# A gated attention with a token mixer, one core: the small row group takes all its weight blocks from transposes

## The chip, the cores and the metric

The kernel runs on one core of a Trainium2 chip. Its engines each work through a list of instructions of their own, in order: TensorE (PE in the profile; its weight loads are listed as PEld), VectorE (DVE), ScalarE (ACT), GpSimd (POOL) and SyncE (SP), which here does nothing but issue DMAs. The metric is the device time of one execution in microseconds (us). Of the kernel before, three executions took 765.38, 765.40 and 765.44 us, with a median of 765.40 us.

## The reference

For each of 8 batches, with S = 3200 tokens and D = 256:

```
scores = (1 / S) * z @ z.T                 # z is 3200 x 64
x      = u * (relu(scores) ** 2 @ v)       # 3200 x 256
wq, wk = x @ w_q, x @ w_k                  # 3200 x 64
mixed  = (1 / 8) * wq @ (wk.T @ x)         # the einsums, in this order of products
out    = relu(mixed) @ w_out               # 3200 x 256
```

The matrix of scores is symmetric, since z is multiplied by its own transpose. The kernel uses this: a block of weights relu(s)^2 between token tiles i and j is the transpose of the block between j and i.

## The kernel before

**Tiles and groups.** The 3200 tokens of a batch are 25 tiles of 128. The rows of the output are taken in seven row groups: groups 0 to 5 have four tiles (512 rows), and the small group, number 6 (`LASTG`), has tile 24 alone (128 rows). For each row group the second product sums over all 25 token tiles: weights block (stationary) times v (moving, 256 columns), into two accumulators `acc` in PSUM, one for the first two row tiles of the group and one for the other two.

**Score tiles and pairs.** A score tile (an entry of the list `tiles`, lines 253 to 281) is 512 columns: for a big group, one token tile against the group's 512 rows; for the small group, four token tiles against its 128 rows, in four matmuls of 128 columns. Two score tiles make a pair. A pair's contraction is 64 long, so its two tiles run side by side, on the upper and the lower 64 rows of TensorE (`scores`, line 296; the matmul is line 307). A pair is then evicted with ReLU and a scale into `g` (`first_stage`: line 321 on DVE, line 319 on ACT), squared into `at` in float16 (`second_stage`: line 332 on POOL, line 330 on ACT), and read by the second product two steps later (`LAG = 2`). There are 11 buffers for `at`, three of two PSUM banks for scores and other short products, and seven for `g`.

**Turned blocks.** Blocks are not computed twice where `is_turned` says so (line 237): for groups gi < gj, with gj at most gi + 2, or the pair (0, 4). Such blocks are computed for group gi, and a DMA transpose from `at` to a shared buffer `tt` (line 351, issued from SP) makes the block that group gj needs. There are seven shared buffers; the plan in lines 285 to 293 gives each new block of groups the buffer whose last read is earliest. For the small group the list `FOR_SMALL` (line 242) names the big groups whose blocks come turned, into buffers of their own, `ts3` to `ts5`; these come from the score tile of token tile 24, which each of the big groups computes anyhow, as the last of its list. The other token tiles of the small group are computed as score tiles of its own: 13 token tiles, so four score tiles of which the last holds tile 24 alone. That makes 114 score tiles in a batch and 912 in all (`NTILE`).

**Steps.** Lines 1028 to 1231 are a loop over numbered steps `k`. A step issues the score matmuls of up to `n = 6` score tiles (three pairs), evicts them, squares the pairs of the step before, and runs a share of the second product of the current row group. The first `heading` pairs are issued at the step's start, the rest between the products. A group takes 25/8, so some three or four steps; the first of them *begins* the group, and the last *closes* it. When a group closes, `gate` (line 488) reads both accumulators: DVE multiplies the first with u (line 507), ACT copies the second to SBUF (line 506), and POOL multiplies that (line 509). The next group's first product into the same accumulators has to wait for that.

**Extra work in a step.** A step can carry one extra piece of the later stages: a *mix* (line 657, in the place of one score pair, so n = 4), a *key* step (`keys_and_heads`, which makes the projections of an x group and the head sums of an older one), or a *projection* (`project`, output products). Where a group begins, the extra piece is put before the group's own first products; elsewhere it goes between them. Which step carries what is decided by rules (`mix_due`, `key_due`, and the condition for `projecting`), and for the steps that stand in the table `chosen` (line 911) by its letters. The table `heading_more` changes the number of heading pairs of a step.

**SP's queue.** SP issues, in one order: loads of u, v and z (v and z come as `piece` in float32, line 147, three buffers, and are cast later by POOL or ACT, line 151, three to five steps after their load), the transposes of x (`xT_sb`, line 518), keys (`kx`, line 551), z (line 176), the turned blocks (line 351) and the stores of the output.

Of the kernel before, what the change touches and what calls it, by code (L numbers as in the profile page):

```python
# [16 lines left out]
def kernel(  # L17
# [219 lines left out]
    def is_turned(gi, gj):  # L237
        return gi < gj < LASTG and (gj <= gi + FAR or (gi, gj) == (0, 4))

    FOR_SMALL = (3, 4, 5)

    def group_of(ti):
        return max(gi for gi in range(NG) if starts[gi] <= ti * P)
# [8 lines left out]
    for b in range(B):  # L254
        for gi in range(NG):
# [4 lines left out]
            if gi == LASTG:  # L260
                own = [t for t in own if group_of(t) not in FOR_SMALL]
            if b == 0 and gi == 0:
# [18 lines left out]
    NTILE = len(tiles)  # L281

    tt_of, tt_free = {}, [(-1.0, n) for n in range(7)]
    for b, gi, tis in tiles:
        gj = group_of(tis[0])
        if is_turned(gi, gj) and (b, gi, gj) not in tt_of:
# [37 lines left out]
    def second_stage(p0, g, on_act):  # L326
# [7 lines left out]
        for h, (b, gi, tis) in enumerate(tiles[p0 : p0 + 2]):  # L334
            for i, ti in enumerate(tis):
                made[b, gi, ti] = (at, h * W + i * widths[gi])
            gj = group_of(tis[0])
            if is_turned(gi, gj) or (gj == LASTG and gi in FOR_SMALL):
                blocks.append((b, gi, gj, tis[0] - starts[gj] // P, 1, h * W, (h + 1) * W))
# [526 lines left out]
    def group_begun(k, b, gi):  # L866
# [40 lines left out]

    heading_more = {165: -1}  # L910
    chosen = {
        18: "k", 19: "p", 20: "p", 21: "m", 35: "k", 36: "p", 38: "p", 101: "p", 142: "mp",
        147: "k", 148: "m", 149: "m", 159: "mp", 161: "p", 163: "m"
    }

    def mix_due(k):
# [72 lines left out]
    def opening(order):  # L989
        sc, g = {}, {}  # L990
        for word in order.split():
            what, n, by = word[0], int(word[1:2]), word[2:]
            if what == "z":
                cast_first(n, int(by[0]), by[1])
            elif what == "t":
                turn_first(n)
            elif what == "c":
                place_first(n, by)
            elif what == "v":
                load_first_v(*[(0, 4), (12, 6), (18, 7), (4, 8)][n])  # L1000
            elif what == "s":
                sc[n] = scores(2 * n)
            elif what == "e":
                g[n] = first_stage(2 * n, sc.pop(n), by == "A")
            elif what == "q":
                each(second_stage(2 * n, g.pop(n), by == "A"))
            elif what == "w":
                warm(2 * int(word[1:]))
            elif what == "u":
                load_u(0, 0)  # L1010
            elif what == "m":
                ti = [t for x in tiles[2 * n : 2 * n + 2] for t in x[2]]
                for fn in whole(second_product(0, 0, ti, n == 0, False)):
                    fn()
        return [(2 * n, g[n]) for n in sorted(g)]
# [3 lines left out]
    waiting = opening(OPENING)  # L1019
    made_by = [4, 10, 16]  # L1020
    produced, consumed, k = 16, 6, 3
# [6 lines left out]
    while groups:  # L1028
# [3 lines left out]
        n = 6  # L1032
# [7 lines left out]
        if mix_due(k):  # L1040
# [1 line left out]
            mixed_at[0] = k  # L1042
            mixing += (mix(*mixing),)
            n = 4
        n = min(n, NTILE - produced)
        pairs = list(range(produced, produced + n, 2))
        on_lanes = k >= 3 and len(pairs) + bool(mixing) >= 2
        keying = not mixing and key_due(k)
# [26 lines left out]
            stage(p0, sc)  # L1075
        if len(waiting) == 3:
            second_on_act = [False, True, k % 2 == 0]
        else:
            second_on_act = [False, True]
        seconds = [(p0, g, a) for (p0, g), a in zip(waiting, second_on_act) if g is not None]  # L1080
# [149 lines left out]
        waiting = staged  # L1230
# [123 lines left out]
```

## Time and profile before

The profiled execution took 765.49 us, of which its span, from the first to the last instruction, is 763.7 us; so some 1.8 us lie around the span, and the execution is 0.09 us above the median.

| engine | busy us | share of the span | instructions |
|---|---|---|---|
| PE | 754.3 | 99% | 12888 |
| ACT | 551.1 | 72% | 651 |
| POOL | 537.1 | 70% | 351 |
| DVE | 461.9 | 60% | 458 |

In the rows that follow, a group of instructions is shown as line, engine, operation, tiles (out<-in), shapes and count; behind the first bar stands the time in which at least one of them ran and the mean of one in ns, behind the second the engine's idle time before them. "64*128" is the part of TensorE's array that a matmul takes, so two such matmuls can run at once. A timeline row gives the start, the length, the engine, the instruction and, in brackets, the idle time before it. In the rows of stretches the first column is the stretch, then its length, and for each engine busy time and instructions, then the granted clock of TensorE, the share of the DMA engines and GB/s.

### The profile page before, as it was taken

How to read it: one execution, taken by the hardware profiler on the slowest of the kernel's cores; microseconds unless marked ns; L12 is line 12 of the kernel's file. 1: busy time of each engine (PE TensorE's matmuls, PEld its weight loads, DVE VectorE, ACT ScalarE, POOL GpSimd, SP SyncE). 2: the span in 40 equal slices, each digit the busy share in tenths (PEclk: the TensorE clock that was granted, in tenths of full speed). 3: DMA queues.
4: the chain of work that ended last, by engine and by line, in shares of the span. 5: the costliest groups of instructions: out<-in, count | busy, mean ns of one | idle time of the engine just before them, and what ended most of it. 6: DMA issues, size and time to landing. Idle time of an engine off the chain costs nothing.

```text
span 763.7 us, 29059 instructions
## 1 busy us (share of the span) xinstructions
PE 754.3 (99%) x12888; PEld 618.0 (81%) x12888; DVE 461.9 (60%) x458; ACT 551.1 (72%) x651; POOL 537.1 (70%) x351
## 2 busy tenths in 40 slices
PE   9999999999999999999999999999999999999996
PEld 6777888888888887888888888888878888888884
DVE  7655676546755567555665557656566565755534
ACT  8666776677767777687776877759777697776555
POOL 7897797768766678676787668866688665854540
PEclk9999999999999999999999999999999999999999
DMA  8999789887999969997899998999899999798636
GB/s 178 189 197 219 187 187 192 174 181 160 206 196 233 219 166 185 221 235 195 214 177 219 243 195 181 158 228 265 135 223 189 228 250 156 161 222 193 176 74 262
DMA packets 289614, 150.23 MB, mean 197 GB/s; under 512 B 265168, under 2 KB 268752, under 8 KB 289488
## 3 DMA queue, kind: packets, MB, share of 16 engines
q1 hardware_dynamic: 288768, 146.48, 91.2%
q0 software_dynamic: 576, 1.64, 1.1%
q8 instruction: 100, 1.64, 0.9%
q14 instruction: 26, 0.21, 0.1%
q10 hardware_dynamic: 144, 0.26, 0.1%
HBM read 59.38 MB, written 26.21 MB: 112 GB/s over the span
## 4 chain that ended last, share of the span: by engine, by line
PE 97%; DVE 2%; issue 0%; DMA 0%; ACT 0%; DVEq 0%; ACTq 0%
PE acc L369 72%; PE sc L307 12%; PE fo L369 5%; PE qk L369 5%; PE mx L657 1%; DVE x_sb L507 1%; DVE fo L1312 0%; DVE g L321 0%; PE ztp L130 0%; DMA z<-in_z_dram 0%; PE qk L610 0%; DVE zT L136 0%; PE xtx L634 0%; PE hd L644 0%; ACT fo L1316 0%
## 5 line engine op out<-in xcount | busy, mean ns | idle before, releaser
L321 DVE TENSOR_SCALAR g<-sc 128x1024 f32<-128x1024 f32 x329 | 400.5, 1223 | 240.5 <-PE sc L307 225.9
L332 POOL TENSOR_TENSOR at<-g 128x1024 f16<-128x1024 f32 x229 | 431.4, 1893 | 131.1 <-DVE g L321 106.5
L369 PE MATMUL acc<-v_sb,at 64*128 64x256 f16 (+1 forms) x7187 | 461.8, 269 | 1.6 <-DVE x_sb L507 0.5
L369 PEld LDWEIGHTS <-at 64*128 64x128 f16 (+1 forms) x7187 | 353.9, 94 | 86.9 <-PE acc L369 25.4
L330 ACT ACTIVATE at<-g 128x1024 f16<-128x1024 f32 x227 | 236.1, 1056 | 14.3 <-DVE g L321 7.2
L369 PE MATMUL acc<-v_sb,tt 64*128 64x256 f16 x2552 | 178.7, 269 | 0.0
L307 PE MATMUL sc<-zT 64*128 64x512 f16 (+1 forms) x1008 | 165.3, 357 | 0.2
L319 ACT ACTIVATE g<-sc 128x1024 f32<-128x1024 f32 x127 | 130.0, 1024 | 45.5 <-PE sc L307 43.2
L369 PEld LDWEIGHTS <-tt 64*128 64x128 f16 x2552 | 130.1, 94 | 14.2
L509 POOL TENSOR_TENSOR x_sb<-gt,u_sb 128x512 f16<-128x512 f32 x48 | 61.2, 1276 | 66.2 <-ACT gt L506 61.8
L678 ACT ACTIVATE rt<-mx 128x1024 f16<-128x1024 f32 x47 | 47.9, 1024 | 32.6 <-PE mx L657 32.5
L506 ACT COPY gt<-acc 128x512 f32<-128x512 f32 x48 | 28.0, 584 | 46.5 <-PE acc L369 44.7
L307 PEld LDWEIGHTS <-zT 64*128 64x128 f16 x1008 | 51.9, 94 | 8.8 <-issue 1.7
L369 PE MATMUL fo<-wo,rt 64*128 64x256 f16 (+1 forms) x696 | 57.9, 270 | 0.0
L544 ACT CAST qk<-qk 128x512 f16<-128x512 f32 x47 | 27.5, 585 | 34.3 <-PE qk L369 31.6
L369 PEld LDWEIGHTS <-rt 64*128 64x128 f16 (+1 forms) x696 | 35.5, 94 | 15.3 <-PE fo L369 6.3
L507 DVE TENSOR_TENSOR x_sb<-acc,u_sb 128x512 f16<-128x512 f32 x48 | 33.2, 691 | 20.3 <-PE acc L369 19.5
L739 ACT ACTIVATE fo<-fo 128x1024 f32<-128x1024 f32 x39 | 39.9, 1024 | 1.9 <-PE fo L369 1.7
L369 PEld LDWEIGHTS <-x_sb 64*128 64x128 f16 x672 | 29.8, 95 | 4.5 <-PE qk L369 0.9
L369 PE MATMUL qk<-kx,x_sb 64*128 64x64 f16 x672 | 32.8, 190 | 0.0
L369 PE MATMUL qk<-xT_sb,wkq 64*128 64x512 f16 (+3 forms) x118 | 25.8, 326 | 0.0
L369 PE MATMUL qk<-xT_sb,wqk 64*128 64x384 f16 (+3 forms) x148 | 24.8, 296 | 0.0
(86 smaller groups left out, 275.2 us busy)
## 6 DMA issues: line engine op xcount, KB each, us to landing
u_sb<-in_u_dram SPq DMA_DIRECT2D x48, 512.0 KB, 5.5
out_dram<-fo SPq DMA_DIRECT2D x43, 512.0 KB, 4.1
piece<-in_v_dram SPq DMA_DIRECT2D x42, 512.0 KB, 5.2
piece<-in_z_dram SPq DMA_DIRECT2D x7, 512.0 KB, 5.2
tt<-at SPq DMA_TRANSPOSE x162, 4.6
out_dram<-fo SPq DMA_DIRECT2D x9, 256.0 KB, 2.9
piece<-in_z_dram SPq DMA_DIRECT2D x7, 288.0 KB, 4.9
u_sb<-in_u_dram SPq DMA_DIRECT2D x8, 128.0 KB, 4.2
```

Of the source, the lines that this page charges most:

```text
L307: nc.tensor.matmul(out=sc[:, h, at : at + w], lhsT=zT[b][half : half + dqk, ds(z_at(b, h) + ti * P, P)], rhs=zT[b][half : half + dqk, ds(z ...
L319: nc.scalar.activation(out=g[:], in_=sc[:], func=RELU, scale=GSCALE)
L321: nc.vector.tensor_scalar(out=g[:], in0=sc[:], scalar1=0.0, scalar2=GSCALE, op0=AOP.max, op1=AOP.mult)
L330: nc.scalar.square(out=out, in_=g[:])
L332: nc.gpsimd.tensor_mul(out=out, in0=g[:], in1=g[:])
L369: return nc.tensor.matmul(out=self.out, lhsT=self.lhsT(rows), rhs=self.rhs(rows), start=start, stop=stop)
L506: nc.scalar.copy(out=upper[:], in_=accs[1][:])
L507: nc.vector.tensor_mul(out=x[:, 0:n], in0=accs[0][:, 0:n], in1=ug[:, 0:n])
L509: nc.gpsimd.tensor_mul(out=x[:, n : 2 * n], in0=upper[:], in1=ug[:, n : 2 * n])
L544: nc.scalar.copy(out=qks[b, gi][:, 0:gw], in_=out)
L678: nc.scalar.activation(out=out, in_=ps[:], func=RELU)
L739: nc.scalar.mul(out=flat_out[:, sl], in_=part, mul=FINAL_SCALE)
```

## The change

`FOR_SMALL` names all six big groups. So the small group's own list of score tiles keeps token tile 24 alone: one score tile instead of four in each batch, 111 in a batch and 888 in all. Three more DMA transposes in each batch, of 128 x 512 each, turn the blocks of groups 0, 1 and 2 into buffers `ts0`, `ts1` and `ts2`; each is issued after the square of that group's pair with token tile 24. The second product of the small group has the same 25 blocks as before, 24 of them from `ts` buffers.

The shared buffers `tt` are six instead of seven.

The tables of steps are others: `chosen` has six entries instead of fifteen, `heading_more` names steps 61 and 37, and a new table `counts` gives step 37 eight score tiles (four pairs) and step 39 four. For the step after one with four pairs there is a line that squares the second and the fourth on ACT.

```diff
-    FOR_SMALL = (3, 4, 5)
+    FOR_SMALL = (0, 1, 2, 3, 4, 5)
...
-    tt_of, tt_free = {}, [(-1.0, n) for n in range(7)]
+    tt_of, tt_free = {}, [(-1.0, n) for n in range(6)]
...
-    heading_more = {165: -1}
+    heading_more = {61: -1, 37: -1}
+    counts = {37: 8, 39: 4}
     chosen = {
-        18: "k", 19: "p", 20: "p", 21: "m", 35: "k", 36: "p", 38: "p", 101: "p", 142: "mp",
-        147: "k", 148: "m", 149: "m", 159: "mp", 161: "p", 163: "m"
+        20: "m", 21: "p", 78: "p", 80: "k", 158: "p", 160: "m"
     }
...
-        n = min(n, NTILE - produced)
+        n = min(counts.get(k, n), NTILE - produced)
...
         if len(waiting) == 3:
             second_on_act = [False, True, k % 2 == 0]
+        elif len(waiting) == 4:
+            second_on_act = [False, True, False, True]
         else:
             second_on_act = [False, True]
```

The loop's own decisions follow from these numbers and the lines above, with no time in them. Carried through for both kernels they give 165 steps (3 to 167) before and 162 (3 to 164) after. The instructions that differ in number are these:

| instruction | before | after |
|---|---|---|
| PE, scores of 128 columns (line 307) | 128 | 32 |
| PE, scores of 512 columns (line 307) | 880 | 880 |
| DVE, ReLU of a pair (line 321) | 329 | 321 |
| ACT, ReLU of a pair (line 319) | 127 | 123 |
| POOL, square of a pair (line 332) | 229 | 218 |
| ACT, square of a pair (line 330) | 227 | 226 |
| SP, DMA transposes ts<-at (line 351) | 24 | 48 |

The other products have the same columns in sum: 48 of half height (64 rows) are replaced by 24 of full height, since the last steps before the end, where all score tiles have been issued, run their products on the whole array. The steps that begin a group carry this extra work:

| a group begins | before | after |
|---|---|---|
| after a big group, with no extra piece | steps 7, 10, 37 | steps 7, 10, 18, 37, 44, 160 |
| after the small group, with no extra piece | steps 41, 104 | steps 41, 82 |
| all others (big groups), with a key or a projection | 42 | 39 |
| the small group itself | 8 | 8 |

## The prediction

> **What bounds the kernel now.** I read the page's busy times first, then the chain that ended last, then the groups of line 307 by their shapes, and last single stretches and timelines.
>
> ```profile
> span 763.7 us, 29059 instructions
> ...
> PE 754.3 (99%) x12888; PEld 618.0 (81%) x12888; DVE 461.9 (60%) x458; ACT 551.1 (72%) x651; POOL 537.1 (70%) x351
> ...
> PE 97%; DVE 2%; issue 0%; DMA 0%; ACT 0%; DVEq 0%; ACTq 0%
> ```
>
> PE is busy for 99% of the span, and 97% of the chain is PE's own work. So PE's stream sets the time, and two things count: how many columns it has to stream, and the few places where it waits. The other engines have 28 to 40% to spare.
>
> **Fewer score matmuls.** The change takes away 96 matmuls of 128 columns, 12 pairs of score tiles.
>
> ```profile
> L307 PE MATMUL sc<-zT 64*128 64x128 f16 x128 | 6.0, 216 | 0.0
> ```
>
> The mean of one, 216 ns, is not its price: two run side by side, and each next pair starts before the last has ended. The price is the distance between starts. Here is such a pair of score tiles, eight matmuls, in a timeline of PE:
>
> ```profile
> 79.87 0.51 PE L369 MATMUL acc<-v_sb,tt 64*128 64x256 f16 x6
> 80.20 0.41 PE L307 MATMUL sc<-zT 64*128 64x128 f16 x8
> 80.45 0.72 PE L369 MATMUL acc<-v_sb,at 64*128 64x256 f16 x10
> ```
>
> From 80.20 to 80.45 the eight hold PE for 0.25 us. The six products before them, of 256 columns, take 79.87 to 80.20, so 0.055 us each; by columns that makes 8 x 0.0275 = 0.22 us. So a pair costs 0.22 to 0.25 us, and 12 pairs 2.6 to 3.0 us. I take 2.7, nearer to the rate by columns, since these short runs lie within a stream that keeps its rate.
>
> One page of the Trainium skill would give more: TensorEngine Tiling (Array Packing), Instruction Overhead, gives each matmul an overhead of about 60 cycles. By that, four on each half take 4 x (128 + 60) cycles, at the 2.4 GHz of Trainium Kernel Development and Optimization (NeuronCore Architecture) 0.31 us a pair, an estimate, and 3.8 us for 12. The row of 0.25 us speaks against it.
>
> **More bare starts.** Where a group begins, its first products wait until the gate of the group before has read both accumulators. Score pairs at the head of the step cover a part of this wait, and an extra piece (key or projection) covers the rest. Six stretches, each one step: a start with a key (step 18), a bare start (37), a middle step without and with a key (38, 39), a start and a middle step with a projection (100, 101).
>
> ```profile
> 77.13:82.44 5.31, 5.31 (x114) 4.78 (x110) 2.95 (x4) 5.03 (x7) 4.11 (x3) 1.00 0.64 179
> 163.33:168.46 5.13, 5.05 (x88) 4.16 (x84) 2.95 (x3) 4.87 (x6) 4.26 (x3) 1.00 0.61 206
> 168.46:172.63 4.17, 4.17 (x80) 3.45 (x76) 2.45 (x2) 4.15 (x5) 3.77 (x4) 1.00 0.36 74
> 172.63:177.55 4.92, 4.92 (x98) 4.28 (x95) 2.65 (x3) 2.91 (x5) 3.61 (x2) 1.00 1.04 237
> 441.43:446.93 5.50, 5.50 (x104) 4.62 (x100) 3.14 (x3) 5.24 (x6) 4.50 (x4) 1.00 1.28 218
> 446.93:451.95 5.02, 5.02 (x96) 4.31 (x92) 2.45 (x2) 2.56 (x4) 3.39 (x2) 1.00 0.61 132
> ```
>
> A key in the middle costs 4.92 - 4.17 = 0.75 us, at a start only 5.31 - 5.13 = 0.18; a projection costs 5.02 - 4.17 = 0.85 in the middle and 5.50 - 5.13 = 0.37 at a start. So a piece that moves from a start to another place costs 0.48 to 0.57 us more, which is the wait that it no longer covers. The wait itself, at step 10:
>
> ```profile
> 36.73 0.60 PE L369 MATMUL acc<-v_sb,tt 64*128 64x256 f16 x8
> ...
> 37.17 0.81 PE L307 MATMUL sc<-zT 64*128 64x512 f16 x6
> 37.40 0.69 DVE L507 TENSOR_TENSOR x_sb<-acc,u_sb 128x512 f16<-128x512 f32 x1 [0.50 <-PE acc L369]
> ...
> 38.06 0.59 PE L369 MATMUL acc<-v_sb,at 64*128 64x256 f16 x7
> ```
>
> Three score pairs hold PE to about 37.83 (6 x 0.11, twice the columns of a product); DVE's gate runs from 37.40 to 38.09, and PE's next product starts at 38.06, with its end. After a big group the old table has three bare starts (7, 10, 37), the new one six (18, 44 and 160 come in). Step 160 puts a mix and two score pairs at its head, which cover as much as three pairs. So 3 x 0.53 = 1.6 us are added, between 1.4 and 1.7. Bare starts behind the small group stay two.
>
> Nothing is priced for the pieces that the table moves otherwise: a middle step costs the same wherever it is, and three steps fewer save no stream. Step 37 with four pairs has three at its head, like before, and the fourth after half of its products, some 2.5 us later, when buffers are free again.
>
> **Less work beside PE.** DVE loses 8 evictions, ACT 4 and one square, POOL 11 squares:
>
> ```profile
> L321 DVE TENSOR_SCALAR g<-sc 128x1024 f32<-128x1024 f32 x329 | 400.5, 1223 | 240.5 <-PE sc L307 225.9
> L332 POOL TENSOR_TENSOR at<-g 128x1024 f16<-128x1024 f32 x229 | 431.4, 1893 | 131.1 <-DVE g L321 106.5
> ```
>
> That is 9.8 us of DVE and 20.8 us of POOL, off the path: worth nothing while PE sets the time.
>
> **More transposes.** SP issues 24 more, three in a batch. Line 351's instructions (ns: least, median, most), then two stretches of SP's queue in batch 5:
>
> ```profile
> L351 SPq DMA_TRANSPOSE tt<-at x162: 1195/1373/4432, 13.1 to 719.6; - x162
> L351 SPq DMA_TRANSPOSE ts<-at x24: 1194/1253/2101, 62.7 to 736.3; - x24
> ```
>
> ```profile
> 504.06 1.27 SPq L551 DMA_TRANSPOSE kx<-qk  x1
> 505.43 5.42 SPq L351 DMA_TRANSPOSE tt<-at  x2
> 510.91 0.57 SPq L147 DMA_DIRECT2D piece<-in_v_dram  x1
> 511.58 2.98 SPq L518 DMA_TRANSPOSE xT_sb<-x_sb  x1
> 514.69 1.57 SPq L351 DMA_TRANSPOSE tt<-at  x1
> ...
> 522.70 0.53 SPq L147 DMA_DIRECT2D piece<-in_v_dram  x1
> ...
> 539.14 1.71 SPq L351 DMA_TRANSPOSE ts<-at  x1
> 543.21 1.17 SPq L551 DMA_TRANSPOSE kx<-qk  x1
> ```
>
> From 504.06 to 516.26 SP issues for 11.81 of 12.20 us: while groups 0 to 3 are scored it has no room. Towards the batch's end it has: from 540.85 to 543.21 it stands idle for 2.36 us in one place. So three transposes, 3 x 1.25 = 3.75 us by the median and 6.3 by the longest, make everything behind them later, and the queue catches up before the next batch. The new blocks themselves are read only when the batch's last group runs, ten steps or more after they are made. What hides the delay is the time between a landing and its first use. At nothing, then, with 0 and 5.6 us (worked out below) as the ends; I take 0, since the waiting would have to pass through two queues before PE sees it.
>
> **Six buffers.** By the plan a block's first transpose now stands, in four places (two in batch 1, two in batch 6), in the step before the last read of that buffer's old block, and in six more in the same step; with seven buffers none did. SP would be held for at most the one step, 4.17 us, and for less, since its queue often runs some 5 us behind anyway (the key of the last rival). Bounds 0 and 4.17 us of SP's time in four places; I take 0.
>
> **The sum.** 763.7 - 2.7 + 1.6 = 762.6 us of span, and with the 1.8 us around it 764.4 against this execution's own 765.49; the median of the runs lies 0.09 us lower, so 764.3 us. That is 1.1 us or 0.14% below 765.40. What a measurement of this kernel can tell from no change is about 0.2%, 1.5 us; so the forecast is "no change that counts", from 763.87 to 766.93, with a small gain inside. Its own range, from the bounds of the two terms (a gain of 0.9 to 1.6 us), is 763.8 to 764.5.
>
> **Rivals.** *The whole gain.* If the added starts find their gate done earlier, because DVE and ACT have fewer evictions ahead of it, the 1.6 us fall away: 762.7 us. For it: after the small group, whose gate is short, a bare start costs less:
>
> ```profile
> 460.65:464.65 4.00, 3.94 (x68) 3.14 (x64) 2.78 (x3) 3.71 (x5) 3.92 (x6) 1.00 0.97 118
> 367.09:371.73 4.64, 4.64 (x84) 3.70 (x80) 2.88 (x3) 4.39 (x6) 3.76 (x4) 1.00 0.77 212
> ```
>
> A projection there adds 0.64 us to a start, so a bare one costs 0.85 - 0.64 = 0.21. Against it: in the rows of step 10 DVE had been idle for 0.50 us before the gate, so it isn't held up by evictions, and fewer of them change nothing. I give it 25%, more than these rows alone would, since the table also moves other pieces that I priced at nothing.
>
> *SP's queue falls behind, and PE feels it: slower.* The place is the cast of v pieces in the middle of a batch.
>
> ```profile
> piece<-in_v_dram SPq DMA_DIRECT2D x42, 512.0 KB, 5.2
> ...
> 528.16 1.04 POOL L151 CAST v_sb<-piece 128x1024 f16<-128x1024 f32 x1
> ```
>
> The piece issued at 522.70 is cast 5.46 us later, and such pieces land after 5.2: 0.26 us to spare. Three transposes more ahead of it make it 3.75 us late, and POOL waits 3.5 us, with a square of 1.89 behind that. A square has about one step, 4.17 us, before it is read: 3.5 + 1.89 - 4.17 = 1.2 us of PE. On ACT, where every other cast runs, the square takes 1.06, so 0.4 us. One of each kind in turn over seven batches: 7 x 0.8 = 5.6 us, 769.9. It decides from a lateness of some 2.5 us on, two transposes. Against it: PE now has no wait for a late `at` worth naming, and POOL was idle for 131.1 us before its squares. 18%.
>
> ```profile
> DMA packets 289614, 150.23 MB, mean 197 GB/s; under 512 B 265168, under 2 KB 268752, under 8 KB 289488
> ...
> ts<-at SPq DMA_TRANSPOSE x24, 4.3
> ```
>
> The Trainium skill (DMA: Bandwidth & Descriptors, Specifications) says that transfers below 512 B don't reach line rate. The trace agrees in kind: most packets are that small, and a transpose of 128 KB (128 x 512 in float16) lands after 4.3 us, a load of 512 KB after 5.2.
>
> *A key or a buffer comes late in a few places.* In the last batch the new table has keys in steps 147 and 149, and the second one's head sums need the first one's transpose. Before, the steps were 146 and 150:
>
> ```profile
> 648.87 0.59 ACT L544 CAST qk<-qk 128x512 f16<-128x512 f32 x1
> ...
> 654.52 1.21 SPq L551 DMA_TRANSPOSE kx<-qk  x1
> ...
> 659.83 0.39 PE L369 MATMUL qk<-kx,x_sb 64*128 64x64 f16 x8
> ```
>
> ```profile
> 650.30:658.86 8.56, 8.56 (x144) 6.65 (x140) 7.16 (x7) 6.80 (x8) 6.86 (x5) 1.00 0.86 174
> ...
> kx<-qk SPq DMA_TRANSPOSE x47, 3.7
> ```
>
> From the cast's end, 649.46, to the first head sum are 10.4 us with three steps of five token tiles between, 8.6 us by their stretch. A token tile's products take (4.17 - 2.85) / 3 = 0.44 us, so the new table's one step between, with six, takes 3.3 us, and its first step, with seven, 0.9 more: 10.4 - 8.6 + 3.3 + 0.9 = 6.0 us. SP was 5.1 us behind, and a key lands after 3.7: at worst PE waits 8.8 - 6.0 = 2.8 us; at best, with only one transpose of 1.2 us ahead, nothing. With the four buffer waits, worth a few tenths each, this is 766 to 768: 12%, half of it within 0.2%.
>
> **Chances and range.** Forecast 45%, of which 5 fall on the fast side of 763.87; whole gain 25; SP's queue 18; late key or buffer 12. So faster 0.30, within 0.2% 0.46, slower 0.24. Below 762.3 (the whole gain with the pair at 0.25 us) I leave 6%, above 769.0, which takes in most of the queue's case, 10%: range 762.3 to 769.0.
>
> **What would show it.** Right: 32 matmuls of 128 columns at line 307 and 48 `ts` transposes; PE's busy time some 1 to 3 us lower at 99%; at steps 18, 44 and 160 PE's `acc` starting with the end of DVE's gate, some 0.4 us after the third pair. For the queue: POOL or ACT waiting for a DMA of `piece`, and PE's weight loads waiting for POOL or ACT at `at`. For the key: weight loads of `x_sb` or products of `kx` waiting for a DMA around the last batch's second group. The forecast is wrong if the starts without a piece don't cost their half microsecond, or if PE's idle time grows anywhere else.

## The result, and the profile after

The changed kernel took 767.55 us (median of 14 runs, 766.90 to 771.42) against 765.52 us for the kernel before (14 runs, 765.38 to 766.52) on the same chip: a ratio of 1.0032, 95% interval 1.0022 to 1.0042. It is slower by 0.3%, where 764.3 us and no change that counts had been forecast. Its profiled execution took 767.29 us. From the page of the changed kernel:

```profile
span 765.4 us, 28850 instructions
...
PE 751.9 (98%) x12768; PEld 616.9 (81%) x12768; DVE 452.7 (59%) x450; ACT 547.7 (72%) x646; POOL 516.8 (68%) x340
...
q1 hardware_dynamic: 301824, 149.63, 96.5%
...
q8 instruction: 100, 1.64, 0.9%
...
PE 93%; POOL 1%; ACT 1%; DVE 1%; issue 1%; DMA 1%; SPq 1%; ACTq 0%; DVEq 0%; POOLq 0%
```

And the DMA queue of SP in the kernel before (packets, MB, share of the 16 DMA engines' time):

```profile
q1 hardware_dynamic: 288768, 146.48, 91.2%
```

PE's busy time fell by 2.4 us (754.3 to 751.9), near the forecast; in a second profile of the same kernel (e9, below) it is 752.8, so the fall is 1.5 us there. PE stands still for 765.4 - 751.9 = 13.5 us, where it was 763.7 - 754.3 = 9.4. So 4.1 us of idle time came in and ate the gain. (Idle time is not the whole of the waiting: step 18 in the next rows loses some 0.5 us with 0.13 us of it idle.) The chain now runs through POOL, ACT, DMA and SP's queue, which it hardly did before. DMA packets take 96.5% of what 16 engines have, after 91.2%.

Where do the 4.1 us lie? First step 10, then the stretches that answer to those of the prediction: step 18 (bare start, now without a key), 37 (four pairs), 39 (two pairs), 44 (bare start), 58 and 59 (a key step that turns the heads, then the first mix of a batch), 76 (as 58), 160 (start with a mix).

```profile
37.15:42.73 5.58, 4.98 (x83) 3.92 (x79) 3.05 (x3) 5.58 (x7) 4.16 (x9) 1.00 1.14 207
77.53:82.67 5.14, 5.01 (x87) 4.15 (x82) 2.95 (x3) 4.84 (x6) 4.22 (x4) 1.00 0.84 118
163.06:168.19 5.13, 5.06 (x87) 4.21 (x83) 4.18 (x4) 4.81 (x6) 4.22 (x3) 1.00 0.96 228
172.35:176.52 4.17, 4.10 (x73) 3.23 (x68) 1.23 (x1) 2.13 (x3) 4.17 (x3) 1.00 1.16 175
195.40:199.64 4.24, 4.05 (x66) 3.09 (x62) 2.96 (x3) 3.42 (x5) 3.27 (x3) 1.00 1.10 146
259.40:265.12 5.72, 5.26 (x105) 4.28 (x100) 2.94 (x4) 3.94 (x7) 4.01 (x3) 1.00 0.78 193
265.12:269.29 4.17, 4.17 (x70) 3.33 (x72) 2.45 (x2) 3.39 (x4) 2.03 (x2) 1.00 0.73 139
339.64:345.36 5.72, 5.25 (x106) 4.28 (x100) 2.94 (x4) 3.88 (x6) 3.90 (x3) 1.00 1.21 246
```

Step 18 takes 5.14 us without its key, as the bare step 37 did before: the term of the bare starts holds (1.6 us for 18, 44 and 160). Step 37 takes the same 5.13 with a fourth pair, and step 39 the same 4.17 with two pairs as a middle step with three, so the table `counts` gives and takes nothing.

New is the end of steps 58 and 76: 0.46 us each in which PE does nothing. PE's timeline there:

```profile
264.37 0.28 PE L610 MATMUL qk<-ident,hT 128*128 128x128 f16 x2
265.12 0.39 PE L657 MATMUL mx<-qk,hs 64*128 64x512 f16 x2 [0.46 <-ACT hs L618]
```

The heads are turned by the last two matmuls of step 58, ACT copies them to `hs` (line 618), and step 59 begins with the mix that reads `hs`. With the old table the first mix of a batch came several steps after the heads; the new table puts it into the very next step, in two places. Each of the two waits is 0.46 us of idle time, so some 0.5 us.

Step 10 is the same in both tables, yet took 5.58 us instead of 5.14 (37.17 to 42.31 before):

```profile
36.05 1.06 ACT L330 ACTIVATE at<-g 128x1024 f16<-128x1024 f32 x1 [4.57 <-DMA tt<-at]
...
37.02 1.00 ACT L319 ACTIVATE g<-sc 128x1024 f32<-128x1024 f32 x1
...
38.07 0.61 PE L307 MATMUL sc<-zT 64*128 64x512 f16 x4 [0.54 <-ACT g L319]
```

Read it from below: PE's second score pair waits 0.54 us for a PSUM buffer that ACT's eviction frees; that eviction stood behind ACT's square; and the square waited for a DMA, since its `at` buffer still had to be read by a transpose, which SP issued at 30.57 us and which landed only at 35.97. The instructions of line 351 after (ns: least, median, most) and who waited for them (us, times), then who waited before:

```profile
L351 SPq DMA_TRANSPOSE ts<-at x48: 1188/1232/2291, 19.0 to 736.2; - x48
...
  POOL at L332: 12.6, 6
  ACT at L330: 12.6, 5
  POOL x_sb L509: 2.4, 1
```

```profile
  ACT at L330: 4.8, 2
```

Last, the end. The first product of the small group now waits for the gate, behind a step of six token tiles instead of eight, and after PE's last product the stores take longer. From the timeline of PE and the DMA view of the stretch from 754 us on, after:

```profile
740.76 0.27 PE L369 MATMUL acc<-v_sb,at 128*128 128x256 f16 x1 [0.19 <-DVE x_sb L507]
...
756.59 1.04 PE L369 MATMUL fo<-wo,rt 128*128 128x256 f16 x8
```

```profile
q8 instruction: 1, 0.02, 0.4%
...
out_dram<-fo SPq DMA_DIRECT2D x5, 256.0 KB, 5.0
```

and before:

```profile
756.03 1.04 PE L369 MATMUL fo<-wo,rt 128*128 128x256 f16 x8
```

```profile
out_dram<-fo SPq DMA_DIRECT2D x4, 256.0 KB, 3.4
```

PE ends at 757.63 instead of 757.07, but the span at 765.4 instead of 763.7: 7.8 us behind PE's end, after 6.6. The stores land 5.0 us after their issue instead of 3.4. And a packet of the instruction queue falls into them, which the same stretch of the kernel before doesn't have. Both kernels load 100 such packets of 16 KB (1.64 MB); that they are PE's list of instructions follows from e5 and e18 below, where some PE instructions less make 99 of them. With 240 instructions less on PE, the last one comes at 757.5 us instead of 741.

So there are three candidates: the queue of transposes, the places of the pieces (starts, mix behind the heads), and the last packet.

### The profile page after: what moved, and what is told of

Same layout as the page of the kernel before. It is cut to its first block, busy times and chain, and to the rows that moved or that the text cites. A ratio compares the mean times of both kernels' runs of the same rounds, so it can differ in the third digit from the quotient of the medians.

```text
span 765.4 us, 28850 instructions
## 1 busy us (share of the span) xinstructions
PE 751.9 (98%) x12768; PEld 616.9 (81%) x12768; DVE 452.7 (59%) x450; ACT 547.7 (72%) x646; POOL 516.8 (68%) x340
## 3 DMA queue, kind: packets, MB, share of 16 engines
q1 hardware_dynamic: 301824, 149.63, 96.5%
q0 software_dynamic: 576, 1.64, 1.1%
q8 instruction: 100, 1.64, 0.9%
## 4 chain that ended last, share of the span: by engine, by line
PE 93%; POOL 1%; ACT 1%; DVE 1%; issue 1%; DMA 1%; SPq 1%; ACTq 0%; DVEq 0%; POOLq 0%
PE acc L369 69%; PE sc L307 11%; PE fo L369 5%; PE qk L369 4%; PE mx L657 1%; POOL at L332 1%; DVE x_sb L507 1%; DMA tt<-at 1%; ACT g L319 1%; DVE fo L1314 0%; PE sc L981 0%; ACT at L330 0%; ACT gt L506 0%; PE qk L610 0%; SPq L195 0%
## 5 line engine op out<-in xcount | busy, mean ns | idle before, releaser
L321 DVE TENSOR_SCALAR g<-sc 128x1024 f32<-128x1024 f32 x321 | 391.0, 1224 | 244.8 <-PE sc L307 232.3
L332 POOL TENSOR_TENSOR at<-g 128x1024 f16<-128x1024 f32 x218 | 410.8, 1893 | 144.6 <-DVE g L321 111.0
L369 PE MATMUL acc<-v_sb,at 64*128 64x256 f16 (+1 forms) x7003 | 449.2, 269 | 2.8 <-DVE x_sb L507 0.9
L369 PEld LDWEIGHTS <-at 64*128 64x128 f16 (+1 forms) x7003 | 345.6, 94 | 86.0 <-PE acc L369 25.2
L369 PE MATMUL acc<-v_sb,tt 64*128 64x256 f16 (+1 forms) x2540 | 178.9, 269 | 0.0
L307 PE MATMUL sc<-zT 64*128 64x512 f16 (+1 forms) x912 | 160.6, 371 | 0.9 <-ACT g L319 0.5
L319 ACT ACTIVATE g<-sc 128x1024 f32<-128x1024 f32 x123 | 125.9, 1023 | 42.9 <-PE sc L307 42.3
L369 PEld LDWEIGHTS <-tt 64*128 64x128 f16 (+1 forms) x2540 | 130.0, 94 | 15.2
L307 PEld LDWEIGHTS <-zT 64*128 64x128 f16 x912 | 49.2, 94 | 9.6 <-issue 2.5
```

The source lines that it names most:

```text
L307: nc.tensor.matmul(out=sc[:, h, at : at + w], lhsT=zT[b][half : half + dqk, ds(z_at(b, h) + ti * P, P)], rhs=zT[b][half : half + dqk, ds(z ...
L319: nc.scalar.activation(out=g[:], in_=sc[:], func=RELU, scale=GSCALE)
L321: nc.vector.tensor_scalar(out=g[:], in0=sc[:], scalar1=0.0, scalar2=GSCALE, op0=AOP.max, op1=AOP.mult)
L332: nc.gpsimd.tensor_mul(out=out, in0=g[:], in1=g[:])
L369: return nc.tensor.matmul(out=self.out, lhsT=self.lhsT(rows), rhs=self.rhs(rows), start=start, stop=stop)
```

## The experiments

A step's loss, in what follows, is its time less what its columns take at PE's pace; in the changed kernel's profile step 58 lost 0.75 us, step 10 lost 1.0, a bare start 0.55 and a middle step mostly under 0.1. All medians are of runs beside the kernel before on the same chip, which stood at 765.39 to 765.47 us throughout. The kernels e1 to e4, e5 to e8, e9 to e12, e13 to e16, and e17 and e18 shared a chip each.

| run | us | lowest to highest |
|---|---|---|
| e1 before, six buffers | 765.58 | 765.20 to 766.34 |
| e2 before, six buffers, 24 transposes more | 766.92 | 766.25 to 769.05 |
| e16 before, 21 transposes more, none in batch 0 | 765.88 | 765.47 to 767.89 |
| e15 before, fewer zero matmuls | 766.70 | 765.16 to 768.01 |
| e9 after, again | 767.54 | 767.00 to 771.04 |
| e3 after, without the 24 transposes | 766.40 | 766.06 to 767.18 |
| e4 after, heads one step earlier | 767.28 | 766.33 to 769.59 |
| e10 after, weights later | 768.34 | 766.36 to 773.81 |
| e5, e6, e7, e8 (one chip) | 769.13, 771.00, 769.09, 771.02 | 766.96 to 773.37 |
| e13 heads, two starts, without the 24 | 765.36 | 764.88 to 766.69 |
| e14 heads, two starts | 766.12 | 764.80 to 770.31 |
| e11 four edits, without the 24 | 765.07 | 764.03 to 766.68 |
| e12 mended | 767.96 | 766.12 to 769.14 |
| e17 mended, batch 0 less turned | 765.76 | 764.71 to 767.41 |
| e18 the same, without the last packet | 765.52 | 764.41 to 766.20 |

### Buffers and transposes

```diff
-    tt_of, tt_free = {}, [(-1.0, n) for n in range(7)]
+    tt_of, tt_free = {}, [(-1.0, n) for n in range(6)]
```

> The kernel before with six shared buffers instead of seven, nothing else. Placement theory (the 2 us come from where the new table puts the pieces: a mix right behind the turned heads, bare starts, the last group): no change, 765.3 to 765.8 us. Queue theory (the 24 transposes more make SP's queue late): no change either. Buffer theory (SP is held where a block's first transpose waits for the old block's last read): slower by 0.5 to 2 us, 766 to 767.5, with issues of tt transposes that start more than 5 us after their data are ready.

765.58 us, ratio 1.0000 (0.9992 to 1.0009). Six buffers cost nothing; the buffer theory falls.

e2 adds the transposes to e1, into a scratch buffer that nothing reads, and e3 takes them out of the changed kernel (first e2's edit, then e3's):

```diff
-            if is_turned(gi, gj) or (gj == LASTG and gi in FOR_SMALL):
+            if is_turned(gi, gj) or (gj == LASTG and gi < LASTG):
...
+                name = f"ts{gi}" if gi in FOR_SMALL else "tx"
...
```

```diff
-            if is_turned(gi, gj) or (gj == LASTG and gi in FOR_SMALL):
+            if is_turned(gi, gj) or (gj == LASTG and gi in (3, 4, 5)):
...
-        return turned[b, gj, gi][rows, j, ti - starts[gj] // P, :]
+        return turned[b, gj + 3 if gi == LASTG and gj < 3 else gj, gi][rows, j, ti - starts[gj] // P, :]
```

> The kernel before with six shared buffers and 24 transposes more: the blocks of groups 0 to 2 with token tile 24 are turned into a scratch buffer that nothing reads; score tiles and table as before. Placement theory: within 0.3 us of the run with six buffers alone, 765.3 to 765.8. Queue theory: slower by most of the 2 us, plus the part that the change's gain hid, 767 to 770, with casts of v pieces or weight loads waiting for DMAs, and a wider spread of the times.

> The changed kernel without the 24 transposes of groups 0 to 2; the small group reads the blocks of groups 3 to 5 in their place, so its rows of the output are others. Placement theory: like the changed kernel, 767.0 to 767.6. Queue theory: 765 to 766, and the spread of the times as narrow as that of the kernel before.

The two mirror each other: e2 is 1.34 us slower than e1, e3 1.15 us faster than the changed kernel, and e3's runs lie within 1.1 us, where the changed kernel's lay within 4.5. So the transposes cost 1.2 to 1.3 us, by median, and in these runs the wider spread goes with them. (The spread alone shows little: the kernel before itself ranged over 1.6 us in 28 runs on the chip of e1 to e4, and over 3.1 in 21 on that of e9 to e12.) That is more than half of the 2.0 us, but not all: e3 still stands 0.95 us above the kernel before, with 2.4 us less to stream. Neither theory alone was right.

In e3's profile step 10 takes 5.14 us again, as in the kernel before. In e4's profile, a run of 769.59 us, the same place is the worst of all:

```profile
37.83 1.06 ACT L330 ACTIVATE at<-g 128x1024 f16<-128x1024 f32 x1 [4.80 <-DMA tt<-at]
...
39.85 0.61 PE L307 MATMUL sc<-zT 64*128 64x512 f16 x4 [2.25 <-ACT g L319]
```

Here PE waits 2.25 us. The new transpose of group 0 (`ts<-at`, at 19.0 us in the changed kernel) stands ahead of the one that ACT waits for, which SP issues at 31.8 us, after 30.6 in the changed kernel and 28.5 in the kernel before.

But the wait at step 10 is not the new transposes' alone. This is e1, which has none of them:

```profile
36.51 1.06 ACT L330 ACTIVATE at<-g 128x1024 f16<-128x1024 f32 x1 [5.01 <-DMA tt<-at]
...
38.53 0.61 PE L307 MATMUL sc<-zT 64*128 64x512 f16 x4 [0.98 <-ACT g L319]
```

SP was as late there, at 30.7 us, by 0.9 us more in its first transposes and 1.3 us more for one load. PE's wait at this place is 0.53 to 0.98 us in the profiles of e1, e11, e13, e15 and e16, which turn no more in the first batch than the kernel before, and it is absent in those of e3 and the kernel before: 0.54 us in the mean of these seven. In the seven that do turn more there and load the weights at the same steps (the changed kernel, e2, e4, e5, e7, e9, e14) it is 0.54 to 2.25 us, 1.16 in the mean. So by the profiles step 10 holds some 0.6 us of the transposes' cost, an estimate from few profiles; where the rest lies is not shown.

e16 asks whether it is the first batch or any: e2's edit, but not in the first batch (`or b > 0 and gi < LASTG`).

> As e2 (six shared buffers, transposes of the blocks of groups 0 to 2 into a scratch buffer that nothing reads), but not in the first batch: 21 transposes more instead of 24. Theory of the early queue: the cost sits at step 10, in the first batch, so the time is that of e1, 765.4 to 765.8. Theory of the whole queue: 21/24 of e2's 1.34 us, 766.5 to 766.9.

765.88 us, ratio 1.0005 (0.9996 to 1.0013), 0.3 us above e1. By the medians, then, 21 transposes cost 0.3 us, and the three of the first batch about 1.0; with intervals of some 0.7 us to either side (e2's ratio is 1.0011 to 1.0030) the split is rough. And the full queue is felt in other places too when the table leaves it less room. In e12's profile it was step 34, in batch 1, by the same path:

```profile
148.73 1.06 ACT L330 ACTIVATE at<-g 128x1024 f16<-128x1024 f32 x1 [6.07 <-DMA ts<-at]
...
150.75 0.39 PE L307 MATMUL sc<-zT 64*128 64x512 f16 x2 [1.53 <-ACT g L319]
```

Two attempts to give SP room ahead of step 10 move the loads of the weights, to ACT's queue (e6) and to later steps (e10):

```diff
-        nc.sync.dma_start(out=raw["q"], in_=moe_w_q.rearrange("(c p) h -> p c h", p=P))
+        nc.scalar.dma_start(out=raw["q"], in_=moe_w_q.rearrange("(c p) h -> p c h", p=P))
...
```

```diff
-    due(6, load_weights)
+    due(10, load_weights)
...
```

> The changed kernel with the three loads of the weights (w_q, w_k, w_out) issued from ACT's queue instead of SP's. Theory of the early queue (the 24 transposes cost their time almost wholly at step 10, where the first of them stands ahead of the transposes that ACT's square waits for): SP is some 1.1 us earlier there, the loss of step 10 falls from 1.0 us to about 0.56, as in the kernel before, the time is 766.2 to 767.1 and its spread narrower. Rival (the transposes cost a little everywhere, by the load of the DMA queue): 767.2 to 767.7 with a spread as before.

> The changed kernel with the loads of the weights issued at steps 10 and 11 instead of 6 and 8, still on SP, their casts at steps 12 and 13. Theory of the early queue: SP is 1.05 us earlier ahead of step 10 (two issues of 0.57 and 0.48 us), which takes back most of what the block of group 0 added (1.2 us); the loss of step 10 falls to 0.56 us, and the time is lower than the control's by 0.4 to 1.2 us. Rival (the transposes cost a little everywhere): within 0.2 us of the control.

Both failed in time. In both profiles step 10 came back to 0.56 us of loss, as expected; but e12, which also loads the weights later, has a wait of 0.98 us there again. In e6 ACT's own list stands still: it issues the first load only at 22.89 us and the second at 23.64, just after two of SP's transposes have landed (22.87 and 23.61), and the square behind them starts at 24.18, where it starts at 19.86 in the changed kernel. PE's next scores wait 2.19 us for the eviction behind that square: step 7 lost 4.6 us, and the time was 771.0 us. In e10 the lateness turned up at step 135 (1.7 us in the profile) and the runs went from 766.4 to 773.8 us, so what it gained is not told from chance. e9 is the control to it:

> The changed kernel unchanged, as a control on this chip beside the next three. If the excess of the changed kernel depends on how fast a chip's DMA is (e5 to e8, on another chip than e1 to e4, were all at 769 to 771 us, with new waits at step 10 and for the key of step 149), it may be anything from 767 to 771 us here, while the kernel before stays at 765.4 to 765.6. If it doesn't depend on the chip: 767.3 to 767.8, and the edits of e5 to e8 themselves cost 1.5 to 3.5 us.

767.54 us, as on the first chip. e5 to e8 ran on another chip without such a control, all with new waits for DMAs; their times are not compared with others here, only their traces are read. Whether the changed kernel itself is slower on that chip stays open.

### Where the table puts the pieces

e4 and e7 each change letters of the table: the heads one step earlier, and pieces moved to bare starts. Both write the table out for all steps; these are the entries that say something else than before.

```diff
...
+        57: "k", 58: "p", 75: "k", 76: "p",
...
```

```diff
...
+        18: "k", 22: "", 43: "", 44: "k", 159: "m", 160: "mp",
...
```

> The changed kernel with steps 57 and 58 exchanged in what they carry (key, then projection), and 75 and 76 in the same way, so that the heads are turned two steps ahead of the first mix of a batch instead of one. Placement theory: PE's wait of 0.63 us before the mix of steps 59 and 77 falls to 0.1 or less; faster by 1.0 us than the changed kernel, 766.2 to 766.8. Queue theory: no change from the changed kernel, 767.3 to 767.8, since SP is as late as there.

> The changed kernel with three pieces moved to the bare starts: a key from step 22 to 18, one from 43 to 44, a projection from 159 to 160. Starts theory (a piece that is moved off a start costs 0.5 us, as predicted): steps 18, 44 and 160 lose 0.05 to 0.1 us instead of 0.55, step 22 gains 0.25; faster by 1.1 to 1.4 us than the changed kernel, 766.1 to 766.5. Rival (most of a bare start's loss is no wait for the gate, but the change of lanes in the middle, which stays): faster by 0.3 to 0.6, 766.9 to 767.3.

In e4 the wait before the mix is gone:

```profile
268.26 0.38 PE L657 MATMUL mx<-qk,hs 64*128 64x512 f16 x2
```

Its median, 767.28 us, gave only 0.3 us, far under the spread of its runs. In e7 the starts 18 and 160 lost less than 0.3 us each, as the starts theory has it. The third didn't: the key at 44 had two pairs ahead of it instead of one, so it waited 1.06 us for a PSUM buffer that ACT had to free. And step 21, the first batch's small group, waited for its last turned block (group 5's, by the time at which SP issued it, so one that the kernel before turns too):

```profile
96.12 0.61 PE L369 MATMUL acc<-v_sb,ts 64*128 64x256 f16 x8 [0.68 <-DMA ts<-at]
```

SP had issued that transpose at 89.27 us, behind a key's and two loads, and it landed 6.8 us later. No other profile here has such a wait. e13 and e14 keep the heads and the starts 44 (with one pair ahead, `44: -1` in `heading_more`) and 160, without and with the 24 transposes.

> The changed kernel without the 24 transposes, as in e3 (the small group's rows of the output are others), with the heads one step earlier (57/58, 75/76), a key at 44 instead of 43 and a projection at 160 instead of 159; the opening is untouched. Placement theory: e3's 766.4 us less 0.9 for the heads (steps 58 and 76 lost 0.37 and under 0.3 in e11, 0.75 each before) and 1.0 for the two starts: 764.3 to 764.8. If the gain is eaten by later waits: 765.5 to 766.4.

> The same table with all 48 transposes. If the two causes add up: 764.5 plus the 1.2 us that the transposes cost in e2 and e3, 765.4 to 766.0, about the kernel before. If the mended table makes the queue's lateness worse, as a key at 18 did in e12: 766.5 to 767.5.

e13 took 765.36 us, 1.0 us less than e3 (1.9 expected); e14 took 766.12 us, ratio 1.0013 (1.0001 to 1.0025), 1.4 us less than the changed kernel (1.9 expected). PE's last product ends at 756.3 and 756.4 us in their profiles, 1.3 us ahead of the changed kernel. So the places of these pieces, the two starts included, were worth 1.0 to 1.4 us, and the two causes add up nearly.

### The last packet of instructions

e5 takes zero matmuls out of the opening, so that the last packet isn't needed. The expectations speak of 19; the profiles have 6 of them instead of 26, so 20 less, 40 PE instructions with their weight loads.

```diff
-        v0 z00D z01A w10 t0 w2 w1 c0D
+        v0 z00D z01A w1 t0 w1 w1 c0D
```

> The changed kernel with 19 zero matmuls less in its opening (each with its weight load, 38 instructions of PE in all). Fetch theory (the changed kernel has 240 PE instructions less, so the last 16 KB packet of the instruction queue, which came at 741 us, now comes at 757.5 us, into the last stores of the output, and holds up one DMA engine's share of them): with 38 instructions less that last packet is not fetched at all; from PE's end to the span's end 6.6 to 6.8 us instead of 7.8, the last stores land 3.4 us after their issue instead of 5.0, and the time is 766.2 to 766.7. Rival (the last stores are late because of what the new table leaves to be stored at the end): 7.7 to 7.9 us, 767.2 to 767.7.

PE's end and the stores, in e5:

```profile
759.70 1.04 PE L369 MATMUL fo<-wo,rt 128*128 128x256 f16 x8
```

```profile
q14 instruction: 1, 0.01, 0.1%
...
out_dram<-fo SPq DMA_DIRECT2D x8, 256.0 KB, 2.3
```

The span ended at 767.1 us, 6.4 us behind PE, and no `q8` packet lies in the stretch; there are 99 in all. This is as the fetch theory has it. Over all 20 profiles of this study the time behind PE's end is 6.3 to 6.9 us in the ten without that packet among the stores (before, e1, e2, e5, e8, e11, e12, e15, e16, e18) and 7.0 to 8.0 in the ten with it, 0.9 us apart in the mean. But the time of e5 was 769.13 us. In its profile PE waits 1.96 us at step 10 and 0.84 us for a late key (below). The edit itself costs time too, as e15 shows in the kernel before:

> The kernel before with the 19 zero matmuls less in the opening. Its last packet of instructions comes some 16 us before the end in any case, so only the opening changes. In two of four profiles with fewer of them (e8 and e11) the first products ran at half their rate for about 1 us. If that is their price: about half of the runs at 766.3 to 766.8, the others at 765.4, so the median of e5, e8, e11 and e12 holds some 0.5 us that are no part of the change. If it was chance: 765.3 to 765.7 with a spread as before.

766.70 us by median, 1.3 us slower: the zero matmuls are needed. The first products in e15, then in the kernel before:

```profile
7.56 1.89 PE L369 MATMUL acc<-v_sb,at 128*128 128x256 f16 x8
```

```profile
7.37 1.05 PE L369 MATMUL acc<-v_sb,at 128*128 128x256 f16 x8
```

The same eight products take nearly twice as long. So they do in e8 and e11; in e5 and e12, with the same edit, they run at the full rate, so the price is paid in some runs only. The Trainium skill (TensorE: Matmul & The Clock Gate, Part 1: The HAM clock gate) says that TensorE runs at half its clock until it has been busy for some 3.4 us. The slow rows agree with that; the granted clock, which reads 1.00 for this stretch in both profiles, does not show it.

### All together

> The changed kernel with all of these edits together: heads one step earlier, covered starts, fewer zero matmuls, weights on ACT's queue; and a key moved from step 83 to the bare start of 82, one from the small group's step 40 to 39. If the losses are separate, their sum comes back: 1.0 + 1.2 + 1.1 + 0.4 to 1.2 us, and 0.3 for the two more, so 762.7 to 763.6 us, faster than the kernel before by 1.8 to 2.7 us. If the losses hide one another (a later wait takes the place of each that is removed): 764.5 to 766.

> The changed kernel without the 24 transposes, as in e3 (the small group reads the blocks of groups 3 to 5 in the place of those of groups 0 to 2, so its rows of the output are others), and with the table mended: heads one step earlier (57/58, 75/76), a key at 18 instead of 40, one at 44 instead of 43, a projection at 160 instead of 159, 19 zero matmuls less in the opening. Placement theory: e3's 766.4 us less 1.0 for the heads, 1.4 for the starts and 1.1 for the last packet of instructions: 762.6 to 763.4, and PE loses less than 0.35 us in every step but 7, 10, 37 and 41. If the table's losses are only moved about: 765 to 766.

> The changed kernel with all 48 transposes, the same mended table, the weights loaded later as in e10, and the key of step 149 moved to 150 (a mix and a projection in 149). If both theories hold, it is slower than e11 by at most 0.5 us: 762.8 to 763.9, faster than the kernel before by 1.5 us or more. If the queue's lateness costs at other places too: 764.5 to 767, with waits of PE, ACT or POOL for a DMA at steps other than 10 and 149.

e8 carries the costs of e6 and e7. e11 and e12 hold the heads, three moves to starts (18, 44, 160) and the shorter opening, e11 without the 24 transposes. e11 took 765.07 us, ratio 0.9989 (0.9980 to 0.9999): the only kernel whose interval lies under the one before, though its profiled opening ran at half rate as in e15. Its lowest runs, 764.0 us, are near the 762.6 to 763.4 that were expected, and its median is not. e12, with all 48 transposes, took 767.96 us, and PE waits in its profile at step 10 (0.98 us), at step 34 (above) and at step 18, where the key that had been put there waited 1.37 us for ACT.

The last two leave the opening alone. e17 is e14 with groups 0 and 1 of the first batch not turned for the small group; e18 also runs step 161's products on the whole array, 60 PE instructions less, so that the last packet falls away.

```diff
-    FOR_SMALL = (0, 1, 2, 3, 4, 5)
+    def for_small(b):
+        return (2, 3, 4, 5) if b == 0 else (0, 1, 2, 3, 4, 5)
```

```diff
-        on_lanes = k >= 3 and len(pairs) + bool(mixing) >= 2
+        on_lanes = k >= 3 and k != 161 and len(pairs) + bool(mixing) >= 2
```

> The kernel of e14 (all of the reference computed), but in the first batch only groups 2 to 5 are turned for the small group, so the two transposes that stand first in SP's queue fall away (46 in all) and one score pair more is computed; the key of step 25 moves to 26, where a group now begins, and step 39 has three pairs. Theory of the early queue: step 10 loses what it loses in the kernel before (0.56 us in its profile), the time is 0.5 to 0.9 us below e14's 766.1, so 765.2 to 765.6, with a narrower spread. Theory of the whole queue: 766.0 to 766.2.

> As e17, with the products of step 161 on the whole array instead of two halves, which are 60 instructions of PE less, so the last 16 KB packet of instructions isn't fetched; the opening is untouched. Fetch theory: from PE's end to the span's end 6.4 to 6.8 us instead of 7.3 to 8.0, and the time 0.5 to 1.1 us below e17's: 764.3 to 764.9, faster than the kernel before by 0.5 to 1.1 us. Rival: step 161 on the whole array loses as much as the last stores gain, within 0.2 us of e17.

765.76 us, ratio 1.0006 (0.9997 to 1.0014), and 765.52 us, ratio 0.9997 (0.9988 to 1.0006). In both profiles step 10 is back at 0.56 us, and in e18 the time behind PE's end is 6.8 us, in e17 7.4. By the medians the last packet gave 0.24 us and not the 0.5 to 1.1 that were expected, close to the rival (within 0.2 us), and the intervals overlap. e18 takes back the changed kernel's loss of 2 us, but doesn't beat the kernel before: step 34 loses 1.1 us in both profiles. Its path differs a little from e12's: a late square on ACT keeps PE waiting first for the weights themselves and then for the eviction behind it. In e17, whose lines are numbered one higher:

```profile
145.71 1.06 ACT L331 ACTIVATE at<-g 128x1024 f16<-128x1024 f32 x1 [5.32 <-DMA tt<-at]
...
146.82 0.39 PE L370 MATMUL acc<-v_sb,at 64*128 64x256 f16 x4 [0.51 <-ACT at L331]
...
147.73 0.39 PE L308 MATMUL sc<-zT 64*128 64x512 f16 x2 [0.30 <-ACT g L320]
```

No version that computes the whole reference came out ahead by more than its interval.

## Why the prediction was wrong

**Fewer score matmuls: right, as far as busy time shows it.** 2.7 us forecast, 2.4 us less busy time in one profile of the changed kernel and 1.5 in the other (e9).

**More bare starts: right.** Three more at 0.5 us each; covered again, 18 and 160 lost under 0.3 us in e7's trace, 44 and 160 in e14's.

**Six buffers: right.** Nothing forecast, 0.1 us measured (e1).

**More transposes: the first step that failed.** "I take 0, since the waiting would have to pass through two queues before PE sees it." It does pass: from SP's queue to the square on ACT, which needs an `at` buffer back, to the eviction behind that square, to PE's scores. The transposes cost 1.15 to 1.34 us (e2, e3), within the bounds of 0 to 5.6. The rival of SP's queue had the cause, but looked in the middle of a batch and at the casts of v pieces; by e16 most of the cost comes with the first batch's three transposes, where the queue is late already. The path is shown at step 10, at which some 0.6 us of the cost lie by the profiles; a wait of the same kind comes there by chance without the new transposes, and the place of the rest stays open. "PE now has no wait for a late `at` worth naming" was true of the kernel before, but ACT's wait was there to be seen before. Its timeline in the kernel before, just ahead of step 10:

```profile
34.67 1.06 ACT L330 ACTIVATE at<-g 128x1024 f16<-128x1024 f32 x1 [3.17 <-DMA tt<-at]
```

It waits 3.17 us for the same transpose as in the changed kernel, short enough to cost PE nothing; 1.4 us more, in the changed kernel (4.57), and it shows.

**Pieces that the table moves otherwise: the second step that failed.** "A middle step costs the same wherever it is." A mix does not, where the heads that it reads were turned in the step before. Some 0.5 us twice in the profile; with the two starts, which the sum had priced, e14 gained 1.4 us, and the heads alone 0.3 by e4's median. A smaller one of its kind is the last big group's closing step with six token tiles, too short to cover the gate: 0.2 us of idle time in the row of 740.76.

**Not in the list at all: the last packet of instructions.** 0.9 us behind PE's end, by the profiles, from 240 instructions of PE less: 96 score matmuls and 24 others with their weight loads, a count that the forecast's own text held. The one pair of runs that tests it with the opening untouched, e17 and e18, gave 0.24 us by median; so the mechanism is in the traces, and its price in time is not settled.

**The late key** of steps 147 and 149 was not seen in the changed kernel's profile. In e5's it was, at step 149, so the mechanism is there when the queue is later still:

```profile
674.88 0.24 PE L369 MATMUL qk<-kx,x_sb 64*128 64x64 f16 x3 [0.84 <-DMA kx<-qk]
```

Forecast and misses add up: 764.3 + 1.2 + 1.0 + 0.2 + 0.9 = 767.6, against 767.55 measured. That the sum is so near is partly chance: the 1.2 is a difference of medians, the other three are read from profiles, and the medians gave less for the heads alone (0.3) and the packet (0.24).

## What to carry to other kernels

An engine that is 28% idle can still be on the path for one instruction: follow each buffer that a DMA reads back to the engine that must refill it, and see what stands behind that engine. In a full DMA queue, more work costs where the queue is late already, here by the medians most of all in the first batch. A wait that is seen in one profile can be there without the change: look for it in profiles of kernels that don't have the change before you charge it. When a table of steps is changed, look at each pair of neighbouring steps in which one makes what the next one reads.

## What was not expected of the hardware

A kernel's list of instructions is itself loaded by DMA: 100 packets of 16 KB for PE's 25,536 matmuls and weight loads (99 with 40 or 60 less), each taking a DMA engine 1.1 us on average (0.9% of what 16 engines have in 765 us). Where the last of them falls among the final stores, the kernel ends 0.9 us later behind PE's last product, in the mean of 20 profiles. And 20 zero matmuls less at the start cost 1.3 us, by the median of e15.
